# The opening of an adaLN transformer block: modulation loaded in 256, 384 and 384 columns, in row halves, and row tiles normalised on VectorE

## The chip, the cores and the metric

One core of a Trainium2 chip runs the whole program. The metric is the device time of one execution in microseconds, median of the runs. The profile's span (first to last instruction) is 1.9 to 2.0 us shorter than the time of the same execution. All executions but the timed runs of the kernel before in the first comparison were also recorded with their span and their mean granted TensorE clock (1.0 is full speed). A "half clock" below is a stretch in which the trace's clock records say 0.5.

## The reference

The block normalises x, modulates it, runs linear attention with 32 heads, adds the result to x, and does the same again around a SwiGLU network. The part that matters here is the start:

```python
mod = (_silu(c) @ w_mod).reshape(c.shape[0], 6, 1, -1)      # w_mod: 1024 x 6144
sa, ca, ga, sb, cb, gb = (mod[:, 0], mod[:, 1], ...)
h = _layernorm(x, axis=-1) * (1 + ca) + sa                  # x: 2048 x 1024
qkv = h @ wqkv                                              # wqkv: 1024 x 3072
```

So before the first useful product with `wqkv`, the kernel needs part of x normalised and transposed, and part of the rows `sa` and `ca`, each of which is a product of a vector with a 1024 x 1024 matrix (2 MB each).

## The kernel before

The first 512 rows of x (four row tiles of 128) and the K part of `wqkv` (`wk`, 2 MB) are worked on chunk by chunk: chunk `cc` is 128 of the 1024 features. Eight PSUM banks take eight accumulation groups, (row tile, half of K's columns). Bank 7 is at first used for the modulation sums, so group 7 has to wait until the last of them has been read.

```python
def load_wme(p):                       # 256 columns of ca, then 256 of sa, all 1024 rows
    for base in (D, 0):
        s_ = slice(base + p * 256, base + (p + 1) * 256)
        nc.sync.dma_start(out=wme[:, :, s_], in_=wm_v[:, :, s_])
...
load_wme(0); load_wk(0, 2); load_wme(1); load_wk(2, 4)       # written one per line
load_wme(2); load_wk(4, 6); load_wme(3); load_wk(6, 7); load_wk(7, 8)
...
def mod_mm(kind, c0, c1):              # kind 0: ca, kind 1: sa; matmuls with one output column
    for cc in range(c0, c1):
        o = (2 * cc) + kind
        col = (0 if kind else D) + cc * P
        for j in range(DC):
            nc.tensor.matmul(bank[7][:, o:o + 1], lhsT=wme[:, j, col:col + P], rhs=scT[:, j:j + 1],
                             start=(j == 0), stop=(j == DC - 1))
def mod_pair(p):
    mod_mm(0, 2 * p, 2 * p + 2)
    mod_mm(1, 2 * p, 2 * p + 2)
    mod_rows(2 * p, 2 * p + 2)         # casts and + 1 on VectorE
...
for p in (1, 2):
    for cc in (2 * p, 2 * p + 1):
        for g in range(7):
            kmm(bank[g], 0, G[g][0], G[g][1], cc)
            if p == 1 and cc == 3 and g == 2:
                mod_pair(2)
                for c_ in range(4, 6):
                    modulate(0, c_, saT, ca1T)
mod_pair(3)
for cc in range(6, 8):
    modulate(0, cc, saT, ca1T)
spread(nc.vector, scT[:])
for cc in range(6):
    kmm(bank[7], 0, G[7][0], G[7][1], cc)
for g in range(8):
    for cc in range(6, 8):
        kmm(bank[g], 0, G[g][0], G[g][1], cc)
    k_evac(bank[g], *G[g])             # then the V groups follow, and so on for 800 us
```

"Warm" matmuls with zero operands fill TensorE's early waits. "Tail" below means the matmuls that can only run after the last modulation block: here 6 for group 7 and 8 x 2 for chunks 6 and 7, 22 in all, at 216 ns from start to start.

## Time and profile before

| | before |
|---|---|
| time, first three runs | 840.97 us (840.03 to 841.25) |
| the profiled execution | 842.11 us, span 840.2 us, mean clock 0.998 |
| first V matmul (end of the opening) | 32.97 us |

First the page: TensorE's share of the span, and the chain that ended last.

```profile
PE 827.6 (99%) x4144; PEld 389.8 (46%) x4224; DVE 354.4 (42%) x663; ACT 155.0 (18%) x291; POOL 78.9 (9%) x147
...
PE 96%; SPq 1%; DMA 1%; issue 1%; DVE 0%; DVEq 0%
```

TensorE is the bound nearly everywhere. Only the opening has room. Next come TensorE's instructions in order of time (start, duration, engine, source line, operation, operands, count; in brackets the idle time before and what ended it). L197 is a warm matmul, L376 the transposes of a row tile, L391 the modulation matmuls, L271 the K matmuls, L286 the first V matmuls.

```profile
7.78 0.62 PE L376 MATMUL bank<-ident,M 128*128 128x128 bf16 x8 [0.90 <-ACT M L240]
...
11.36 0.62 PE L376 MATMUL bank<-ident,M 128*128 128x128 bf16 x8 [0.64 <-ACT M L240]
11.81 1.03 PE L271 MATMUL bank<-M,M 128*128 128x512 bf16 x3
...
17.04 2.33 PE L271 MATMUL bank<-M,M 128*128 128x512 bf16 x10 [0.24 <-DVE M L253]
19.23 0.55 PE L391 MATMUL bank<-scT,M 128*128 128x1 bf16 x16
20.96 0.55 PE L391 MATMUL bank<-scT,M 128*128 128x1 bf16 x16 [1.18 <-DMA M<-in_w_mod_dram]
...
26.95 0.94 PE L391 MATMUL bank<-scT,M 128*128 128x1 bf16 x32
28.22 4.91 PE L271 MATMUL bank<-M,M 128*128 128x512 bf16 x21 [0.34 <-DVE saT L396]
32.97 7.29 PE L286 MATMUL bank<-M,M 128*128 128x512 bf16 x33
```

The longest wait is 1.18 us, for the third modulation block, whose second transfer landed at 20.92 us. The last group of 21 shown K matmuls (22 were issued; the record of one is missing) is the tail. Then the granted clock: the windows view gives, for each stretch, busy time by engine, and then the granted clock, the share of the DMA engines and GB/s.

```profile
core 0: us, PE busy (x) PEld busy (x) DVE busy (x) ACT busy (x) POOL busy (x), PEclk, DMA share, GB/s
...
20.00:24.00 4.00, 2.82 (x23) 1.30 (x25) 1.10 (x5) 0.00 (x0) 0.00 (x0) 0.76 1.17 306
24.00:28.00 4.00, 3.89 (x43) 2.05 (x42) 0.06 (x1) 0.00 (x0) 0.00 (x0) 0.82 0.99 336
```

The clock is below 1 from 20 to 28 us. The clock records say it exactly: 0.5 from 22.05 us for 3.41 us, and 1.0 for the rest.

The end of the chain of waits:

```profile
826.02 11.11 PE bank L581 x106
```

### The profile page before, as it was taken

The numbers are of one execution on the slowest core, as the hardware profiler recorded it, in microseconds if no ns is written. First come the engines' busy times: TensorE is split into PE (matmuls) and PEld (weight loads), VectorE is DVE, ScalarE is ACT, GpSimd is POOL, SyncE is SP. The second block draws the span as 40 slices with busy tenths as digits, with TensorE's granted clock in tenths as the row PEclk, the third lists the DMA queues.
The fourth block names the chain that finished last, engine by engine and source line by source line (L and its number), as shares of the span: only waits on it lengthen the run. The fifth ranks groups of instructions, "written<-read, shape, count | busy, mean of one in ns | idle before, by whom it ended". The sixth has DMA issues, their size and how long they took to land.

```text
span 840.2 us, 10541 instructions
## 1 busy us (share of the span) xinstructions
PE 827.6 (99%) x4144; PEld 389.8 (46%) x4224; DVE 354.4 (42%) x663; ACT 155.0 (18%) x291; POOL 78.9 (9%) x147
## 2 busy tenths in 40 slices
PE   7999999999999999999999999999999999999998
PEld 3454554544444444444444444444444444444445
DVE  4668888788655656635341111111101211111111
ACT  4335533323211111111110001111000111100000
POOL 2034210022122323100000000000000000000000
PEclk9999999999999999999999999999999999999999
DMA  9985879055599889777874225555322555211210
GB/s 289 312 165 103 161 139 237 17 151 134 127 225 221 219 233 292 187 251 226 249 245 140 76 69 151 151 151 151 106 75 82 154 157 153 76 36 46 76 69 26
DMA packets 223009, 128.62 MB, mean 153 GB/s; under 512 B 76016, under 2 KB 209136, under 8 KB 222960
## 3 DMA queue, kind: packets, MB, share of 16 engines
q1 hardware_dynamic: 182112, 98.58, 43.0%
q10 hardware_dynamic: 38544, 20.98, 11.1%
q0 software_dynamic: 2304, 8.39, 2.6%
q8 instruction: 33, 0.54, 0.3%
q14 instruction: 16, 0.13, 0.1%
HBM read 97.52 MB, written 12.58 MB: 131 GB/s over the span
## 4 chain that ended last, share of the span: by engine, by line
PE 96%; SPq 1%; DMA 1%; issue 1%; DVE 0%; DVEq 0%
PE bank L562 23%; PE bank L581 23%; PE bank L556 23%; PE bank L513 7%; PE bank L286 7%; PE bank L294 7%; PE bank L271 6%; DMA M<-in_w_mod_dram 1%; PE bank L486 1%; PE bank L303 1%; SPq L148 1%; SPq L145 0%; SPq L140 0%; PE bank L391 0%; PE bank L345 0%
## 5 line engine op out<-in xcount | busy, mean ns | idle before, releaser
L562 PE MATMUL bank<-M,M 128*128 128x512 bf16 x881 | 210.4, 379 | 0.9
L556 PE MATMUL bank<-M,M 128*128 128x512 bf16 x870 | 209.5, 379 | 1.3
L564 DVE TENSOR_TENSOR M<-bank,e 128x512 bf16<-128x512 f32 x112 | 77.4, 691 | 249.3 <-PE bank L562 240.8
L581 PE MATMUL bank<-M,M 128*128 128x512 bf16 (+2 forms) x717 | 147.4, 362 | 0.7
L559 ACT ACTIVATE e<-bank 128x512 f32<-128x512 f32 x112 | 66.8, 598 | 436.2 <-PE bank L556 393.7
L581 PEld LDWEIGHTS <-M 128*128 128x128 bf16 x952 | 90.9, 98 | 102.9
L562 PEld LDWEIGHTS <-M 128*128 128x128 bf16 x896 | 87.7, 98 | 105.7
L556 PEld LDWEIGHTS <-M 128*128 128x128 bf16 x896 | 87.3, 98 | 103.8
L584 DVE TENSOR_TENSOR M<-bank,M 128x512 bf16<-128x512 f32 (+2 forms) x34 | 22.4, 660 | 169.9 <-PE bank L581 169.9
L271 PE MATMUL bank<-M,M 128*128 128x512 bf16 x247 | 58.1, 386 | 1.6 <-DVE M L253 0.6
L513 PE MATMUL bank<-M,M 128*128 128x512 bf16 x254 | 57.8, 379 | 0.1
L294 PE MATMUL bank<-M,M 128*128 128x512 bf16 x250 | 56.7, 379 | 0.3
L286 PE MATMUL bank<-M,M 128*128 128x512 bf16 x251 | 55.8, 379 | 0.3
L266 ACT ACTIVATE e<-bank 128x512 f32<-128x512 f32 x64 | 37.3, 596 | 90.2 <-PE bank L294 50.2
L581 PE MATMUL bank<-M 128*128 128x512 bf16 x218 | 50.3, 379 | 0.2
L268 DVE SCALAR_TENSOR_TENSOR M<-bank,e 128x512 bf16<-128x512 f32 x64 | 44.3, 691 | 3.9
L267 DVE TENSOR_SCALAR e<-e 128x512 f32<-128x512 f32 x64 | 29.4, 460 | 23.0 <-ACT e L266 23.0
L271 PEld LDWEIGHTS <-M 128*128 128x128 bf16 x256 | 24.7, 99 | 30.8 <-issue 2.3
L286 PEld LDWEIGHTS <-M 128*128 128x128 bf16 x256 | 25.0, 98 | 30.0
L513 PEld LDWEIGHTS <-M 128*128 128x128 bf16 x256 | 25.0, 98 | 29.7
L294 PEld LDWEIGHTS <-M 128*128 128x128 bf16 x256 | 24.6, 98 | 27.9
L325 DVE CUSTOM_DVE_ANT_0 M<-M,sc_bc 128x1024 f32<-128x1024 bf16 x24 | 29.8, 1241 | 0.5
(84 smaller groups left out, 357.8 us busy)
## 6 DMA issues: line engine op xcount, KB each, us to landing
M<-in_B_w_gate_dram SPq DMA_DIRECT2D x56, 512.0 KB, 3.9
M<-in_B_w_up_dram SPq DMA_DIRECT2D x56, 512.0 KB, 5.1
x_scratch<-M POOLq DMA_DIRECT2D x16, 512.0 KB, 5.8
M<-x_scratch ACTq DMA_DIRECT2D x16, 512.0 KB, 3.4
M<-in_B_w_down_dram SPq DMA_DIRECT2D x6, 1024.0 KB, 8.1
M<-in_A_x_dram SPq DMA_DIRECT2D x16, 256.0 KB, 3.8
M<-in_w_mod_dram SPq DMA_DIRECT2D x8, 512.0 KB, 7.8
M<-in_A_wqkv_dram SPq DMA_DIRECT2D x4, 1024.0 KB, 10.3
```

What stands on the lines that cost most here:

```text
L266: nc.scalar.activation(out=e[:], in_=acc, func=ACT.Exp)
L268: nc.vector.scalar_tensor_tensor(out=dst, in0=acc, scalar=0.0, in1=e[:], op0=ALU.max, op1=ALU.add)
L271: nc.tensor.matmul(acc[:], lhsT=M4[:, sc_, cc, t * P:(t + 1) * P], rhs=wk[:, cc, h * NB:(h + 1) * NB], start=(cc == 0), stop=(cc == DC - 1))
L286: nc.tensor.matmul(acc[:], lhsT=M4[:, sc_, cc, t * P:(t + 1) * P], rhs=wv[:, cc, h * NB:(h + 1) * NB], start=(cc == 0), stop=(cc == DC - 1))
L294: nc.tensor.matmul(acc[:], lhsT=wq[:, cc, qc * P:(qc + 1) * P], rhs=M4[:, sc_, cc, :], start=(cc == 0), stop=(cc == DC - 1))
L325: nc.vector.tensor_tensor_reduce(out=prod.rearrange("p (j k) -> p j k", j=DC), in0=rowT[i][:, :, b, :], in1=sc_bc[:].rearrange("p (j k) -> ...
L513: nc.tensor.matmul(acc[:], lhsT=oTs[st % 3][:, cc, :], rhs=wo[:, cc, hs], start=(cc == 0), stop=(cc == DC - 1))
L556: nc.tensor.matmul(g_ps[:], lhsT=wg_blk[:, cc, fs], rhs=M4[:, sc_, cc, :], start=(cc == 0), stop=(cc == DC - 1))
L559: nc.scalar.activation(out=sg[:], in_=g_ps[:], func=ACT.Silu)
L562: nc.tensor.matmul(u_ps[:], lhsT=wu_blk[:, cc, fs], rhs=M4[:, sc_, cc, :], start=(cc == 0), stop=(cc == DC - 1))
L564: nc.vector.tensor_tensor(out=gus[sc_][:, f, :], in0=u_ps[:], in1=sg[:], op=ALU.mult)
L581: nc.tensor.matmul(y_ps[:, 0:w], lhsT=gus[sc_][:, f, t * P:(t + 1) * P], rhs=wd(f)[:, c0:c1], start=(f == 0), stop=(f == FC - 1))
```

## The change

The intent is to get the modulation in sooner. After the first block of 256 columns come two of 384 (packets of 768 bytes in place of 512, one block fewer), each in two halves of the rows, and the first half is summed while the second still comes in. Row tiles 1 to 3 are normalised on VectorE, which is faster at it than ScalarE, and the PSUM evacuations of row tiles 0 to 2 go to ScalarE.

```diff
+    PH = [(0, 2), (2, 5), (5, 8)]
-    def load_wme(p):
+    def load_wme(p, j0, j1):
         for base in (D, 0):
-            s_ = slice(base + p * 256, base + (p + 1) * 256)
-            nc.sync.dma_start(out=wme[:, :, s_], in_=wm_v[:, :, s_])
+            s_ = slice(base + PH[p][0] * P, base + PH[p][1] * P)
+            nc.sync.dma_start(out=wme[:, j0:j1, s_], in_=wm_v[:, j0:j1, s_])
...
-    load_wme(0)
+    load_wme(0, 0, DC)
     load_wk(0, 2)
-    load_wme(1)
-    load_wk(2, 4)
-    load_wme(2)
-    load_wk(4, 6)
-    load_wme(3)
-    load_wk(6, 7)
-    load_wk(7, 8)
+    load_wme(1, 0, 4)
+    load_wme(1, 4, 8)
+    load_wk(2, 3)
+    load_wk(3, 5)
+    load_wme(2, 0, 4)
+    load_wme(2, 4, 8)
+    load_wk(5, 6)
+    load_wk(6, 8)
...
+    ln_xn(1, nc.vector)          # and tiles 2 and 3 likewise; before: on ScalarE
...
+    kblk(range(7), 2)
+    kblk(range(7), 3)
+    kblk(range(3), 4)
+    mod_mm(2, 0, 0, 4)           # block, kind, rows: first row half
+    mod_mm(2, 1, 0, 4)
+    kblk(range(3, 7), 4)
+    mod_mm(2, 0, 4, 8)           # second row half
+    mod_mm(2, 1, 4, 8)
+    mod_finish(2)
+    modulate_phase(2)
     spread(nc.vector, scT[:])
-    for cc in range(6):
-        kmm(bank[7], 0, G[7][0], G[7][1], cc)
+    for cc in range(5):
+        kblk((7,), cc)
     for g in range(8):
-        for cc in range(6, 8):
-            kmm(bank[g], 0, G[g][0], G[g][1], cc)
+        for cc in range(5, 8):
+            kblk((g,), cc)
         k_evac(bank[g], *G[g])
```

The tail grows: 5 for group 7 and 8 x 3 for chunks 5 to 7, 29 matmuls in place of 22. With halves, several sums are open in bank 7 at once, and only the first matmul of a block carries the start flag. That the sums come out right this way no run tested by itself; the results of the changed kernel (after_again) and of the nine experiments built on it were correct.

More of the change, by code (lines that the diff above doesn't have):

```diff
@@ L196, in warm @@
         for _ in range(n):
-            nc.tensor.matmul(bank[7][:], lhsT=zt[:, 0:P], rhs=zt, start=True, stop=True)
+            nc.tensor.matmul(bank[3][:], lhsT=zt[:, 0:P], rhs=zt, start=True, stop=True)
     stat = {}
@@ L232, in ln_stats_act, with ln_xn @@
         stat[st] = (rstd, nmr)
-    def ln_xn(st, pool):
+    def ln_xn(st, eng=None):
         rstd, nmr = stat.pop(st)
-        if pool:
-            nc.gpsimd.tensor_scalar(out=xns[st % 6], in0=xs[st % 6], scalar1=rstd[:], scalar2=nmr[:],
-                                    op0=ALU.mult, op1=ALU.add)
+        if eng is not None:
+            eng.tensor_scalar(out=xns[st % 6], in0=xs[st % 6], scalar1=rstd[:], scalar2=nmr[:],
+                              op0=ALU.mult, op1=ALU.add)
         else:
@@ L246, in ln @@
             ln_stats(st)
-        ln_xn(st, True)
+        ln_xn(st, nc.gpsimd)
         sc_, t = divmod(st, STC)
@@ L380, in tr0_evac @@
         dst = M4[:, 0, :, st * P:(st + 1) * P]
-        if st % 2 == 0:
+        if st < 3:
             nc.scalar.copy(out=dst, in_=tp)
@@ L384, in tr0_evac, with mod_mm @@
             nc.vector.tensor_copy(out=dst, in_=tp)
-    def mod_mm(kind, c0, c1):
-        for cc in range(c0, c1):
-            o = (2 * cc) + kind
-            col = (0 if kind else D) + cc * P
-            for j in range(DC):
+    def mod_mm(p, kind, j0, j1):
+        c0, c1 = PH[p]
+        for j in range(j0, j1):
+            for cc in range(c0, c1):
+                o = (2 * cc) + kind
+                col = (0 if kind else D) + cc * P
                 nc.tensor.matmul(bank[7][:, o:o + 1], lhsT=wme[:, j, col:col + P], rhs=scT[:, j:j + 1],
-                                 start=(j == 0), stop=(j == DC - 1))
+                                 start=(not kind and j == 0 and cc == c0),
+                                 stop=(kind == 1 and j == DC - 1 and cc == c1 - 1),
+                                 skip_group_check=True)
     def mod_rows(c0, c1):
@@ L397, in mod_rows, with mod_finish, modulate_phase @@
         nc.vector.tensor_scalar_add(out=ca1T[:, c0:c1], in0=m1[:, 1, c0:c1], scalar1=1.0)
-    def mod_pair(p):
-        mod_mm(0, 2 * p, 2 * p + 2)
-        mod_mm(1, 2 * p, 2 * p + 2)
-        mod_rows(2 * p, 2 * p + 2)
-    warm(17)
-    for st in range(STC):
-        ln_stats(st)
+    def mod_finish(p):
+        mod_rows(*PH[p])
+    def modulate_phase(p, c0=0, c1=SCW):
+        for cc in range(*PH[p]):
+            modulate(0, cc, saT, ca1T, c0, c1)
+    warm(19)
     mask = const.tile([P, KVW], BF16, name="mask")
@@ L413 @@
     nc.gpsimd.memset(v_c[:, :, :, P:VW], 1.0)
-    ln_xn(0, False)
+    for st in range(3):
+        ln_stats(st)
+    ln_xn(0)
     tr0(0)
-    warm(3)
-    ln_xn(1, False)
-    tr0(1)
-    tr0_evac(0)
-    ln_xn(2, False)
-    ln_xn(3, False)
+    tr0_evac(0)
+    warm(2)
+    ln_xn(1, nc.vector)
+    tr0(1)
+    tr0_evac(1)
+    ln_stats(3)
+    mod_mm(0, 0, 0, DC)
+    mod_mm(0, 1, 0, DC)
+    warm(3)
+    mod_finish(0)
+    modulate_phase(0, 0, 2 * P)
+    for st in (2, 3):
+        ln_xn(st, nc.vector)
     load_cols(wv, 2 * D, 0)
@@ L427, with kblk @@
     load_cols(wq, 0, 1)
-    tr0_evac(1)
-    mod_pair(0)
+    G = [(t, h) for t in range(STC) for h in range(NH)]
+    def kblk(gs, cc):
+        for g in gs:
+            kmm(bank[g], 0, G[g][0], G[g][1], cc)
+    kblk(range(4), 0)
     tr0(2)
     tr0_evac(2)
-    for cc in range(2):
-        modulate(0, cc, saT, ca1T, 0, 2 * P)
-    G = [(t, h) for t in range(STC) for h in range(NH)]
-    for cc in range(2):
-        for g in range(4):
-            kmm(bank[g], 0, G[g][0], G[g][1], cc)
-        if cc == 0:
-            tr0(3)
-            tr0_evac(3)
-            for c_ in range(2):
-                modulate(0, c_, saT, ca1T, 2 * P, 4 * P)
-    for cc in range(2):
-        for g in range(4, 7):
-            kmm(bank[g], 0, G[g][0], G[g][1], cc)
-        if cc == 0:
-            mod_pair(1)
-            for c_ in range(2, 4):
-                modulate(0, c_, saT, ca1T)
-    for p in (1, 2):
-        for cc in (2 * p, 2 * p + 1):
-            for g in range(7):
-                kmm(bank[g], 0, G[g][0], G[g][1], cc)
-                if p == 1 and cc == 3 and g == 2:
-                    mod_pair(2)
-                    for c_ in range(4, 6):
-                        modulate(0, c_, saT, ca1T)
-    mod_pair(3)
-    for cc in range(6, 8):
-        modulate(0, cc, saT, ca1T)
+    kblk(range(2), 1)
+    tr0(3)
+    tr0_evac(3)
+    kblk(range(2, 4), 1)
+    modulate_phase(0, 2 * P, 4 * P)
+    mod_mm(1, 0, 0, 4)
+    mod_mm(1, 1, 0, 4)
+    kblk(range(4, 7), 0)
+    mod_mm(1, 0, 4, 8)
+    mod_mm(1, 1, 4, 8)
+    mod_finish(1)
+    modulate_phase(1)
+    kblk(range(4, 7), 1)
+    kblk(range(7), 2)
[8 more added lines that the diff above has]
+    modulate_phase(2)
     spread(nc.vector, scT[:])
-    for cc in range(6):
-        kmm(bank[7], 0, G[7][0], G[7][1], cc)
+    for cc in range(5):
+        kblk((7,), cc)
     for g in range(8):
-        for cc in range(6, 8):
-            kmm(bank[g], 0, G[g][0], G[g][1], cc)
+        for cc in range(5, 8):
+            kblk((g,), cc)
         k_evac(bank[g], *G[g])
```

## The prediction

> **What bounds the kernel now.** The page shows TensorE busy 99% of 840.2 us, and the chain that ended last is 96% TensorE. The waits view shows no TensorE wait after 33 us. So only the opening can move: from 0 to 32.97 us, when the first V matmul starts (TensorE timeline). There the DMA queue runs full (about 290 to 390 GB/s in every microsecond from 3 us on, by the windows view) and TensorE waits in small pieces: 0.90 and 0.27 us (normalised x), 0.64 us (row 2 on ScalarE), 0.38 and 0.24 us (modulation on VectorE), then 1.18 us at 19.8 to 20.96 for the third modulation block. From 22.05 to 25.46 us the granted clock is 0.5, one stretch of 3.41 us that costs 3.41/2 = 1.7 us of TensorE work. The stretch just before it held that wait and N=1 matmuls. [...]
>
> **What changes.**
> 1. Modulation columns 256+256+256+256 become 256+384+384, each 384 in two row halves. DMA packets grow from 512 to 768 bytes. Landings before: 256-column blocks take 3.4 to 4.5 us per MB, wk with 2 KB packets 2.8 us per MB, wv with 1 KB packets 3.0. I estimate 3.25 us per MB for 768 bytes: 3 MB of modulation save about 1.8 us. The last modulation byte lands at about 23.0 to 23.7 us (before: 25.72), the last wk at about 25.3 (before: 27.09).
> 2. After the last landing only 24 N=1 matmuls remain (0.6 us), since the first half was summed already. The K tail after them is 5+24 matmuls at 216 ns = 6.3 us (before: 6+16 = 4.75 us): more tail, but no work in front of it waits.
> 3. Row tiles 1 to 3 are normalised on VectorE: ScalarE takes 1.24 us per tile; on VectorE I estimate 0.54 us, from modulation 0.344 us at 256 and 0.410 us at 512 columns. Evacuations 0 to 2 go to ScalarE (0.99 us), 3 to VectorE (0.69 us). Stats of row 3 now come after row 1's normalisation, so the first modulation still ends near 11.5 to 11.8 us. First K matmul: 11.5 to 11.8 us, before 11.81. No gain there.
> 4. Warm matmuls 20 become 24, in gaps, free. One set of casts and adds less (0.4 us of VectorE), not critical.
>
> **Sum.** After: block 1 finished about 16.6 us, K blocks dense from 17.5 us, second half of block 2 ends about 23.3, bank 7 free about 23.8, 29 matmuls to about 30.2 to 30.5 us. Before: 32.97. Gain 2.3 to 2.7 us against the profiled run, if the half clock disappears: about 1.2 us of it is the clock stretch, the rest earlier landings and the vanished 1.18 us wait. Where runs of before escape the half clock, before would be limited by the landing at 25.72 and the gain is about 1.5 us. Everything after is TensorE-bound and merely moves forward.
>
> **Prediction.** 838.7 us, 80% range 837.2 to 840.4. Faster by over 2%: 0.3%; within 2%: 99%; slower: 0.7%.
>
> **What would show it.** First V matmul at 30 to 31 us; no clock record of 0.5 after 6 us; no TensorE wait over 0.8 us on the modulation load; last modulation landing under 24 us; VectorE normalisation about 0.54 us; TensorE still without waits after 33 us.
>
> **What would make it wrong.** 768-byte packets no faster per byte; a half-clock stretch in the after run (more N=1 matmuls lie together, and its tiles wait around 14 to 17 us); the wait for bank 7 between block 2's reads and the last K group; the K evacuations or the wv load (before landed 29.99 us) now too late for the earlier V groups.

## The result

| | before | changed |
|---|---|---|
| time, median of 6 runs each | 840.62 us (840.03 to 841.25) | 839.83 us (839.22 to 840.41) |
| the profiled execution | 842.11 us, span 840.2, clock 0.998 | 839.79 us, span 837.9, clock 1.000 |
| first K matmul | 11.81 us | 11.53 us |
| last modulation transfer lands | 25.72 us | 23.78 us |
| first V matmul | 32.97 us | 30.86 us |

The ratio is 0.999, with a 95% interval of 0.9977 to 1.0003. The two profiled executions differ by 842.11 - 839.79 = 2.3 us, the medians by 0.8 us.

The page of the changed kernel:

```profile
PE 827.3 (99%) x4148; PEld 390.2 (47%) x4228; DVE 354.6 (42%) x662; ACT 153.2 (18%) x289; POOL 79.5 (9%) x147
...
PE 96%; SPq 2%; DMA 1%; issue 1%; DVE 0%; DVEq 0%
```

TensorE's timeline. Lines have moved: L200 warm, L379 transposes, L395 modulation, L274 K, L289 V.

```profile
7.71 0.62 PE L379 MATMUL bank<-ident,M 128*128 128x128 bf16 x8
...
11.53 1.04 PE L274 MATMUL bank<-M,M 128*128 128x512 bf16 x4 [0.25 <-DVE M L256]
...
15.36 0.59 PE L274 MATMUL bank<-M,M 128*128 128x512 bf16 x2 [0.46 <-DVE M L256]
...
17.62 3.84 PE L274 MATMUL bank<-M,M 128*128 128x512 bf16 x17 [0.24 <-DVE M L256]
21.30 0.74 PE L395 MATMUL bank<-scT,M 128*128 128x1 bf16 x24
...
22.76 0.44 PE L395 MATMUL bank<-scT,M 128*128 128x1 bf16 x12
23.82 0.45 PE L395 MATMUL bank<-scT,M 128*128 128x1 bf16 x12 [0.62 <-DMA M<-in_w_mod_dram]
24.60 6.42 PE L274 MATMUL bank<-M,M 128*128 128x512 bf16 x28 [0.32 <-DVE saT L402]
30.86 9.44 PE L289 MATMUL bank<-M,M 128*128 128x512 bf16 x43
```

The wait for the last block is 0.62 us now, and the tail (28 of its 29 matmuls recorded) takes 6.4 us in place of 4.9. The windows view of the changed kernel shows a full clock:

```profile
core 0: us, PE busy (x) PEld busy (x) DVE busy (x) ACT busy (x) POOL busy (x), PEclk, DMA share, GB/s
...
20.00:24.00 4.00, 3.31 (x53) 2.10 (x53) 0.00 (x0) 0.00 (x0) 0.00 (x0) 1.00 1.08 354
24.00:28.00 4.00, 3.68 (x28) 1.77 (x25) 2.84 (x9) 1.38 (x3) 0.00 (x0) 1.00 1.10 362
```

And the end of the chain:

```profile
823.91 11.11 PE bank L595 x106
```

Subtract the first V matmul from the start of this last chain piece: 826.02 - 32.97 = 793.05 us before, 823.91 - 30.86 = 793.05 us after. From the first V matmul on, the two executions agree to 10 ns. The same sum, taken from each of the 14 traces (first V matmul to the end of TensorE's last), lies between 804.14 and 804.19 us. So nothing is given back later. The time of the first V matmul tells everything about a run but what follows TensorE's last matmul (the last evacuation and store), which took 2.8 to 3.1 us.

### The profile page after: what moved, and what is told of

Its sections match the earlier page's. It is cut to its first block, busy times and chain, and to the rows that moved or that the text cites. A ratio compares the mean times of both kernels' runs of the same rounds, so it can differ in the third digit from the quotient of the medians. Undisturbed runs are those within 1.5% of the kernel's fastest.

```text
span 837.9 us, 10535 instructions
## 1 busy us (share of the span) xinstructions
PE 827.3 (99%) x4148; PEld 390.2 (47%) x4228; DVE 354.6 (42%) x662; ACT 153.2 (18%) x289; POOL 79.5 (9%) x147
## 3 DMA queue, kind: packets, MB, share of 16 engines
q0 software_dynamic: 2304, 8.39, 2.6%
## 4 chain that ended last, share of the span: by engine, by line
PE 96%; SPq 2%; DMA 1%; issue 1%; DVE 0%; DVEq 0%
PE bank L576 23%; PE bank L595 23%; PE bank L570 23%; PE bank L527 7%; PE bank L289 7%; PE bank L297 7%; PE bank L274 6%; DMA M<-in_w_mod_dram 1%; PE bank L500 1%; PE bank L306 1%; SPq L147 1%; SPq L150 1%; SPq L140 0%; PE bank L348 0%; DVE M L361 0%
## 5 line engine op out<-in xcount | busy, mean ns | idle before, releaser
L274 PE MATMUL bank<-M,M 128*128 128x512 bf16 x248 | 56.6, 379 | 1.7 <-DVE M L256 1.0
L289 PE MATMUL bank<-M,M 128*128 128x512 bf16 x251 | 55.8, 379 | 0.3
L289 PEld LDWEIGHTS <-M 128*128 128x128 bf16 x256 | 25.0, 98 | 30.0
L274 PEld LDWEIGHTS <-M 128*128 128x128 bf16 x256 | 24.3, 98 | 29.3 <-DVE M L256 1.8
```

What stands on the lines that cost most here:

```text
L274: nc.tensor.matmul(acc[:], lhsT=M4[:, sc_, cc, t * P:(t + 1) * P], rhs=wk[:, cc, h * NB:(h + 1) * NB], start=(cc == 0), stop=(cc == DC - 1))
L289: nc.tensor.matmul(acc[:], lhsT=M4[:, sc_, cc, t * P:(t + 1) * P], rhs=wv[:, cc, h * NB:(h + 1) * NB], start=(cc == 0), stop=(cc == DC - 1))
```

## The experiments

Twelve experiments ran, each for five timed rounds beside the kernel before, on three chips; all were correct. The two theories at the start:

- Theory 1: the profiled execution of the kernel before was an unlucky one with a half clock. At full clock the changed kernel gains little, because the opening ends at the last modulation landing plus the tail, and the tail grew by 7 x 0.216 = 1.5 us while the landing came earlier.
- Theory 2: the half clock is the rule in the kernel before, and the changed kernel gives its gain back later. (The equal 793.05 us speak against the second half already.)

### before_again: the kernel before once more

The edit is none.

> The kernel before, unchanged, as a control. Theory 1 (the profiled execution of before, 842.11 us, was an unlucky one with a half-clock stretch, and most executions have none): most runs lie at 840.0 to 841.3 us, a profile that shows no clock record of 0.5 after 6 us has its first V matmul at about 31.5 us (landing of the last modulation block 25.7 + 0.2 of its matmuls after it + 0.8 for casts and the freeing of bank 7 + 22 matmuls at 216 ns = 4.75) and not at 32.97. Theory 2 (the half clock is in most executions of before, and the change's gain is given back later): the profile shows the 0.5 stretch again and the first V matmul at about 33 us. Ratio to before 1.000 within 0.001.

The median was 841.09 us (840.25 to 842.58), ratio 1.0009 (0.9997 to 1.0022). The profile fell on a full-clock execution of 840.25 us:

```profile
20.47 0.55 PE L391 MATMUL bank<-scT,M 128*128 128x1 bf16 x16 [0.66 <-DMA M<-in_w_mod_dram]
...
24.96 1.02 PE L391 MATMUL bank<-scT,M 128*128 128x1 bf16 x32
26.32 4.91 PE L271 MATMUL bank<-M,M 128*128 128x512 bf16 x21 [0.34 <-DVE saT L396]
31.07 9.23 PE L286 MATMUL bank<-M,M 128*128 128x512 bf16 x41
```
```profile
core 0: us, PE busy (x) PEld busy (x) DVE busy (x) ACT busy (x) POOL busy (x), PEclk, DMA share, GB/s
20.00:24.00 4.00, 3.45 (x29) 1.69 (x31) 1.10 (x5) 0.00 (x0) 0.00 (x0) 1.00 1.17 306
24.00:28.00 4.00, 3.61 (x45) 2.10 (x44) 1.70 (x6) 0.00 (x0) 0.00 (x0) 1.00 1.08 356
```
```profile
824.16 11.11 PE bank L581 x106
```

Here the third block's second transfer landed at 20.42 us instead of 20.92, the wait was 0.66 us instead of 1.18, the clock stayed full, and the V matmuls started at 31.07 us, 1.9 us earlier than in the first profile. Both traces have nearly the same phase of the clock records (first record at 4.98 and 4.94 us), so the phase is not what differs; the visible difference is half a microsecond in the landing of that transfer. That it decided the clock is argued from this one pair of traces. The V matmuls are also 0.4 us earlier than Theory 1 had put them, which comes up again below.

All executions of the kernel before that were recorded with span and clock are 41. In 28 of them the clock is 0.999 or 1.000, with spans of 838.3 to 839.1 us, median 838.6. Eight have 0.998 and spans of 840.2 to 840.6. Five have 0.997 or 0.998 and yet 838.7 to 838.9; where their clock was lower no trace shows. Theory 1 holds on this point: the half clock that makes an execution 1.6 to 2.0 us longer than that median struck 8 of 41 executions, and the first profile, which is not among the 41, was one such.

### after_again: the changed kernel once more

The edit is none.

> The changed kernel, unchanged, for a closer interval on one chip with the others. Theory 1: ratio to before 0.9985 to 0.9995, that is 0.4 to 1.2 us less, first V matmul at 30.5 to 31.3 us, no half clock, no TensorE wait after 33 us. Theory 2: the same opening, but TensorE waits or a lower clock later in the run that the kernel before has not.

Median 839.84 us (839.47 to 841.69), ratio 0.9995 (0.9981 to 1.0009), first V matmul at 30.89 us. Of the 11 recorded executions of the changed kernel ten have a clock of 1.000, with spans of 837.3 to 838.5, median 837.9; one has 0.998 and 839.8. So at full clock the changed kernel is ahead by 838.6 - 837.9 = 0.7 us in the medians. On the chip of this submission alone it is 838.5 - 837.75 = 0.75 us. The interval of the ratio includes 1; a single half clock in five runs is larger than the gain. In the two full-clock traces before_again and changed the gain of the opening alone is 31.07 - 30.86 = 0.2 us.

### before_fill: the wait before the half clock, filled

```diff
     def mod_pair(p):
         mod_mm(0, 2 * p, 2 * p + 2)
+        if p == 2:
+            for _ in range(5):
+                nc.tensor.matmul(bank[7][:, 32:NB], lhsT=zt[:, 0:P], rhs=zt[:, 32:NB], start=True, stop=True)
```

> The kernel before with five warm matmuls of 480 columns (about 1.0 us at full clock) between the two kinds of the third modulation pair, where TensorE waited 1.18 us. Theory 1: the wait shrinks to under 0.3 us, no clock record of 0.5 after 6 us, first V matmul at 31.3 to 31.8 us; the time equals that of before within 0.5 us, since most executions of before have no half clock to lose. Theory 2: it is 1.0 us or more faster than before.

Median 840.56 us (840.29 to 840.97), ratio 1.000 (0.9988 to 1.0013), first V matmul at 31.15 us, no 0.5 record before the end, and the wait of 1.18 us is gone. All five executions were at 0.999 or 1.000. This agrees with Theory 1 and contradicts Theory 2: without the half clock the kernel before takes what its median execution takes. It does not show that the fill is what kept the clock: at 8 in 41, five executions in a row escape by chance about one time in three (an estimate). The first V matmul came 0.15 us earlier than expected.

### whole_rows: no row halves

```diff
-    load_wme(1, 0, 4)
-    load_wme(1, 4, 8)
+    load_wme(1, 0, DC)
...
-    mod_mm(2, 0, 0, 4)
-    mod_mm(2, 1, 0, 4)
     kblk(range(3, 7), 4)
-    mod_mm(2, 0, 4, 8)
-    mod_mm(2, 1, 4, 8)
+    mod_mm(2, 0, 0, DC)
+    mod_mm(2, 1, 0, DC)
```

(Block 1 and the load of block 2 likewise.)

> The changed kernel without row halves: each 384-column block is loaded in two transfers of all rows and summed when both have landed. Theory 1: the landing of the last block stays at 23.5 to 24.2 us; after it come 24 N=1 matmuls of the second kind instead of 12, 0.3 us more, so the first V matmul is at 31.0 to 31.5 us, 0.2 to 0.6 us later than in the changed kernel. A rival, that the halves are what brought the gain: first V matmul at 31.7 us or later, no gain left against before.

Median 840.42 us (840.2 to 841.17), ratio 0.9999 (0.9987 to 1.0012). The profile fell on the one execution of five with a half clock (17.65 to 21.06 us), with the first V matmul at 31.99 us, so it cannot be compared with the changed kernel's. The other four executions have spans of 838.3 to 838.6, median 838.5: 0.6 us longer than the changed kernel's 837.9, at the upper edge of the expectation. The last landing was at 23.73 us as expected. An estimate from the spans (838.5 less 804.15 and about 2.95 us) puts the first V matmul at full clock at about 31.4 us, short of the rival's 31.7. But the rival's other mark was met: beside the full-clock executions of the kernel before in the same submission, also 838.5, no gain is left. Taken out of the changed kernel, the halves are worth about 0.6 us. (The parts do not add up: the wide blocks and the VectorE move, taken out in the same way below, cost 0.4 to 0.6 us each, though the whole change gains 0.7 us. So none of the parts can be called the one that gains.)

### norm_act: row tiles 1 to 3 on ScalarE

```diff
-    ln_xn(1, nc.vector)
+    ln_xn(1)
...
     for st in (2, 3):
-        ln_xn(st, nc.vector)
+        ln_xn(st)
```

> The changed kernel with row tiles 1, 2 and 3 normalised on ScalarE again. Theory 1 (the opening ends at the last modulation landing plus a tail of fixed length): the first K matmul slips from 11.5 to about 12.6 us and block 1 is summed about 0.6 us later, but TensorE's wait of 0.6 to 0.7 us for the last landing at about 23.8 us takes it up: first V matmul at 30.8 to 31.3 us, time within 0.4 us of the changed kernel where the clock stays full. A half-clock stretch is likelier, since TensorE idles about 1 us more between 9.6 and 13 us. The rival (the move to VectorE is what gains): first V matmul at 31.8 us or later without a half clock.

Median 841.57 us (841.47 to 842.03), ratio 1.0009 (0.9995 to 1.0023). All five executions had a clock of 0.998, so the half clock was not only "likelier" but came every time, and my main number (30.8 to 31.3 us) failed: the first V matmul was at 32.41 us.

```profile
10.58 0.62 PE L379 MATMUL bank<-ident,M 128*128 128x128 bf16 x8 [1.81 <-ACT M L243]
...
13.09 1.91 PE L274 MATMUL bank<-M,M 128*128 128x512 bf16 x4
...
32.41 1.89 PE L289 MATMUL bank<-M,M 128*128 128x512 bf16 x8
```

TensorE waits 1.81 us for row tile 1, because ScalarE first evacuates row tile 0 and then normalises (1.24 us against 0.54 us on VectorE). From 11.60 to 15.01 us the clock record is 0.5. Two causes are mixed in this run, the later start and the clock; a later run, told next, parts them.

### norm_fill: the same, but that wait filled

```diff
-    warm(2)
+    warm(10)
```

> The changed kernel with row tiles 1 to 3 on ScalarE, as in the earlier run, but ten warm matmuls in place of two in the wait for row tile 1 (1.8 us), so that this wait earns no half clock. Theory 3 (what the move to VectorE is worth is the full clock, since the later start alone is taken up by the wait for the last landing): no half clock in most executions, first V matmul at 30.8 to 31.4 us, 1.0 us or more earlier than the 32.41 without the fill, span 837.8 to 838.5. Its rival (the later start is lost time by itself): first V matmul at 31.8 us or later at full clock.

Median 840.2 us (840.11 to 840.71), ratio 0.9991 (0.9977 to 1.0005), all five clocks 1.000.

```profile
8.23 2.32 PE L200 MATMUL bank<-M 128*128 128x512 bf16 x10
10.64 0.62 PE L379 MATMUL bank<-ident,M 128*128 128x128 bf16 x8
...
12.96 1.04 PE L274 MATMUL bank<-M,M 128*128 128x512 bf16 x4 [0.25 <-DVE M L256]
...
31.34 2.97 PE L289 MATMUL bank<-M,M 128*128 128x512 bf16 x13
```

With the wait filled, the first V matmul comes at 31.34 us, 1.07 us before norm_act's and 0.48 us after the changed kernel's. The K matmuls started 12.96 - 11.53 = 1.43 us later, so about 1 us of the late start is taken up by waits further on (the changed kernel's 0.62 us for the last landing is gone from this trace). Since norm_act had the half clock in five of five and this kernel in none, the filled wait is what earned it there. Theory 3, as stated there, holds: most of what the move to VectorE is worth is the full clock, and only 0.4 to 0.5 us is the earlier start.

### blocks256: four blocks of 256 columns, with halves

```diff
-    PH = [(0, 2), (2, 5), (5, 8)]
+    PH = [(0, 2), (2, 4), (4, 6), (6, 8)]
```

(Loads, sums and the tail of 6 + 16 follow from it.)

> The changed kernel with four blocks of 256 columns, row halves kept. Theory 1: the last landing comes later, at 25.2 to 25.6 us, as in the kernel before, but 22 instead of 29 matmuls follow it: landing 25.4 + 0.25 of sums + 0.5 to free bank 7 + 4.75 = 30.7 to 31.1 us for the first V matmul, the same as the changed kernel within 0.3 us: the wider blocks won nothing in net. The rival (larger packets and the earlier landing are what gains): first V matmul 1.5 us or more later than in the changed kernel.

Median 840.34 us (840.31 to 840.58), ratio 0.9993 (0.998 to 1.0005), all five clocks 1.000, first V matmul at 31.17 us, last landing at 25.38 us.

```profile
25.56 0.54 PE L397 MATMUL bank<-scT,M 128*128 128x1 bf16 x16
26.42 4.91 PE L276 MATMUL bank<-M,M 128*128 128x512 bf16 x22 [0.32 <-DVE saT L404]
31.17 3.19 PE L291 MATMUL bank<-M,M 128*128 128x512 bf16 x14
```

The last landing is 1.6 us later than in the changed kernel, and the opening ends only 0.3 us later. The span medians differ by 838.5 - 837.9 = 0.6 us (measured on different chips). So the wide blocks do not bring the 1.6 us of their earlier landing: what they win at the landing they mostly lose in the longer tail. The rival, 1.5 us or more, is refuted.

### mid512 and mid512_fill: the small block last

If landing plus tail were all, blocks of 256, 512 and 256 columns should win on both counts.

```diff
-    PH = [(0, 2), (2, 5), (5, 8)]
+    PH = [(0, 2), (2, 6), (6, 8)]
```

> The changed kernel with blocks of 256, 512 and 256 columns: the last block is small again, so 22 matmuls follow it, while 2 MB of the 4 still move in packets of 768 bytes or more. Theory 1: block 1 is summed by about 17.6 us, 42 K matmuls then keep TensorE busy to about 24.3 us, the last landing is at 23.8 to 24.5 us, and the first V matmul comes at 29.5 to 30.1 us; time 0.8 to 1.4 us less than the changed kernel. If the tail did not matter: first V matmul at 30.9 us or later.

Median 840.26 us (839.99 to 840.89), ratio 0.9993 (0.9981 to 1.0006). Two of five executions had 0.998, the profile among them (first V matmul 31.97 us). The three at full clock have spans of 838.1 to 838.4, no better than the changed kernel, where I had expected 0.8 to 1.4 us less. One fault was mine: the K weights of chunks 3 to 5 were one transfer, which landed at 21.30 us. The second kernel mends that and the half clock:

```diff
-    load_wk(3, 6)
+    load_wk(3, 4)
+    load_wk(4, 6)
...
     mod_mm(1, 0, 4, 8)
+    fill(4)        # zero weights, start=False, onto a running K sum: adds nothing
     mod_mm(1, 1, 4, 8)
```

> Blocks of 256, 512 and 256 columns again, with two mends: the K weights of chunks 3 to 5 are loaded as 3 and then 4 and 5 (in the earlier trace the three together landed at 21.3 us, while TensorE could have used the first at 19.2), and four matmuls with zero weights, which add nothing to a running sum, lie in the wait for block 1's last transfer, where the half clock was earned. Theory 1 (last landing plus tail, once the clock is full): no clock record of 0.5, last landing at 23.8 to 24.7 us, first V matmul at 29.9 to 30.6 us, time 0.3 to 0.9 us less than the changed kernel, all clocks 1.0. If the first V matmul is again at 31 us or later at full clock, the tail is not what counts and theory 1 is wrong for this kernel.

Median 839.96 us (839.69 to 840.42), ratio 0.9987 (0.9975 to 1.000), all five clocks 1.000. The last landing was at 24.36 us as expected, but the first V matmul of the profiled execution, the slowest of the five, at 31.56 us:

```profile
19.50 5.35 PE L275 MATMUL bank<-M,M 128*128 128x512 bf16 x24 [0.24 <-DVE M L257]
24.69 0.54 PE L396 MATMUL bank<-scT,M 128*128 128x1 bf16 x16
...
25.96 0.54 PE L396 MATMUL bank<-scT,M 128*128 128x1 bf16 x16
26.82 4.91 PE L275 MATMUL bank<-M,M 128*128 128x512 bf16 x22 [0.32 <-DVE saT L403]
31.56 2.75 PE L290 MATMUL bank<-M,M 128*128 128x512 bf16 x12
```

TensorE did not wait for the last block: the block landed at 24.36 us, and TensorE reached its first sums at 24.69 us and the last at 25.96 us. From 19.50 us on it worked without a pause but for the 0.3 us for bank 7. So Theory 1's "landing plus tail" is wrong as a general rule. It describes the changed kernel, where TensorE waits for the last landing; in this one TensorE itself is late, because block 1 (2 MB here) landed only at 17.99 us.

### last512: the large block last

```diff
-    PH = [(0, 2), (2, 5), (5, 8)]
+    PH = [(0, 2), (2, 4), (4, 8)]
```

> The reverse: blocks of 256, 256 and 512 columns, so 4 + 32 = 36 matmuls follow the last block. Theory 1: the landing is at 23.4 to 24.2 us, no earlier than in the changed kernel by more than 0.4, and the first V matmul comes at 31.9 to 32.7 us, 1.0 to 1.8 us later than in the changed kernel, and TensorE waits 2 us or more for the last block, so that a half clock in some executions adds up to 1.7 us.

Median 842.26 us (840.88 to 842.52), ratio 1.0012 (1.0000 to 1.0025). Four of five executions had 0.998 (spans 840.1 to 840.6), one 0.999 (839.0). Here TensorE waits for the block (landed 22.99 us, earlier than I had expected) and the tail of 36 matmuls follows from 23.93 us; the profiled execution had its half clock from 23.28 to 26.69 us, and its first V matmul at 33.04 us. An estimate for full clock is 23.93 + 36 x 0.216 = 31.7 us. The wait shown before the last transfer's sums is 0.95 us, half of what I had expected.

### after_fill: the changed kernel with its two waits filled

```diff
     mod_mm(1, 1, 0, 4)
+    fill(2)
...
     mod_mm(2, 0, 4, 8)
+    fill(2)
     mod_mm(2, 1, 4, 8)
```

> The changed kernel with two zero-weight matmuls in each of its two waits of about half a microsecond (before the first use of row tile 3, and before the last modulation transfer). Only the clock should change: no execution at 0.998, spans 837.5 to 838.3 as the full-clock executions of the changed kernel had, which showed one of 0.998 and 839.8 in five on the first chip.

Median 839.87 us (839.65 to 840.01), ratio 0.9986 (0.9973 to 0.9998), all five clocks 1.000, spans 837.8 to 838.1. It is as fast as the changed kernel at full clock. Five runs are too few to show that it never falls to the half clock, where the changed kernel did once in 11.

### last128: an attempt to beat both

```diff
-    PH = [(0, 2), (2, 5), (5, 8)]
+    PH = [(0, 2), (2, 5), (5, 7), (7, 8)]
```

(With the fill of row tile 3's wait, and with two K matmuls moved behind each last sum.)

> An attempt at a kernel that beats both: blocks of 256, 384, 256 and 128 columns in the changed kernel, two zero-weight matmuls in the wait for row tile 3, and only 7 + 8 = 15 matmuls after the last block instead of 29. TensorE work from the first K matmul (11.5 us) adds up to about 17.1 us, so 28.6 us is the earliest possible end of the opening. Theory 1 (landing plus tail, with TensorE's own work as a floor): if the 128-column block (packets of 256 bytes) lands by 26 us, the first V matmul comes at 30.0 to 30.6 us and the time is 0.3 to 0.9 us less than the changed kernel's. If packets of 256 bytes cost much more per byte, the landing passes 26.5 us and the gain is gone. The rival that the tail is not what counts: no earlier first V matmul although the landing is by 26 us.

Median 840.25 us (839.76 to 840.9), ratio 0.9992 (0.9979 to 1.0006), all clocks 1.000. The last block landed at 25.41 us, inside the condition, and yet the first V matmul came at 31.06 us:

```profile
11.83 1.04 PE L275 MATMUL bank<-M,M 128*128 128x512 bf16 x4 [0.25 <-DVE M L257]
...
26.42 0.54 PE L396 MATMUL bank<-scT,M 128*128 128x1 bf16 x16
26.82 3.87 PE L275 MATMUL bank<-M,M 128*128 128x512 bf16 x17
31.06 3.18 PE L290 MATMUL bank<-M,M 128*128 128x512 bf16 x14 [0.36 <-DVE M L272]
```

TensorE reached the last block's sums at 26.42 us, one microsecond after they could have run. Then the tail was so short that two new waits appeared: the first V group needs bank 0, which VectorE was still reading (0.36 us of idle, L272), and the V weights, which landed at 30.89 us against 28.77 us in the changed kernel. It does not beat the changed kernel. None of my versions does, beyond the noise.

### What the traces have in common

A count of TensorE's work between the first K matmul and the first V matmul: 64 K matmuls at 0.216 us, 96 modulation matmuls at 0.025 us and the transposes at 0.056 us each (start to start, from the trace). It is an estimate, and it can be set beside the measured stretch:

```
trace (full clock)   first K   first V   stretch   work counted   rest
before_again          11.88     31.07     19.19     16.7            2.5
after                 11.53     30.86     19.33     17.1            2.2
blocks256             11.53     31.17     19.64     17.1            2.5
norm_fill             12.96     31.34     18.38     17.1            1.3
mid512_fill           12.15     31.56     19.41     17.1            2.3
after_fill            11.42     31.07     19.65     17.1            2.5
```

(The changed kernel transposes one row tile more after its first K matmul, hence 17.1 and not 16.7; mid512_fill and after_fill have 4 fill matmuls, 0.9 us, in their rest.) By this estimate the whole opening can win about 2 us at most after the first K matmul, at full clock, and the rest consists of three or four short waits: for row tile 3, for the casts and the modulation of a block, for the landing, for bank 7. TensorE waits about as long for a landing as before (0.66 us for the third block in before_again, 0.62 us for the last one now), and the other waits moved about. That TensorE's own work is the floor was argued from these counts; no run took work away from it.

## Why the prediction was right or wrong

The measured 839.83 us lies in the stated range of 837.2 to 840.4, 1.1 us above the point. By the points:

- "Everything after is TensorE-bound and merely moves forward": right, to 10 ns (793.05 us in both).
- "First K matmul: 11.5 to 11.8 us": right, 11.53. The VectorE estimate of 0.54 us: right, 0.541 us. The 3.25 us per MB for 768-byte packets: right, the 384 KB transfers landed 1.20 us apart, 3.2 us per MB.
- "The last modulation byte lands at about 23.0 to 23.7 us": 23.78 us. The transfer of K weights before it took 2.1 us instead of 1.4.
- "29 matmuls to about 30.2 to 30.5 us": 30.86 us, 0.4 us late, from that landing.
- "Gain 2.3 to 2.7 us against the profiled run": 2.3 us between the profiled executions, 2.1 us in the first V matmul, so right or just short. Its split was wrong, so part of this is luck: 1.9 of the 2.1 us is the difference between two executions of the kernel before (32.97 and 31.07), where I had put 1.2 us on the clock, and 0.2 us is the change. The step that failed is the next one: the point of 838.7 is that gain subtracted from 840.97 us, the median of the timed runs, although the profiled run, with its half clock, was at 842.11 us. Subtracting the gain from its own base gives 842.11 - 2.3 = 839.8 us, which is what was measured. before_again, before_fill and the count of 8 in 41 show that the half clock belongs to that execution and not to the kernel.
- "Where runs of before escape the half clock ... the gain is about 1.5 us": mis-sized. It is 0.2 us in the two full-clock traces, and 0.7 us in the medians of the full-clock spans. The term that was wrong is the end of the full-clock opening before: I put it at about 31.8 us, it was 31.07, since its last landing came at 25.38 and TensorE got to the block at 24.96, just in time. With 22 matmuls behind it, 25.38 + 5.69 = 31.07; with 29, 23.78 + 7.08 = 30.86: of the 1.6 us of earlier landing, 1.4 us went into the longer path after it. The sums hold in other full-clock traces: before_fill 25.46 + 5.69 = 31.15 (measured 31.15), after_again 23.82 + 7.08 = 30.90 (30.89), after_fill 23.99 + 7.08 = 31.07 (31.07). For the first profile the sum gives 25.72 + 5.69 = 31.4 (an estimate), so of its 1.9 us some 1.6 us is the half clock and 0.3 us a later landing. I had noted the longer tail, but wrote that "no work in front of it waits", while in fact TensorE waited 0.62 us for the landing.
- That the half clock comes from waits and small matmuls was right as far as norm_act and norm_fill test it: with ScalarE doing the normalising in the changed kernel it strikes five of five, and with the wait filled none. Whether the change lowers the risk is not shown: 1 of 11 executions against 8 of 41 is too few to tell.
- That 839.83 us fell inside the range says little for the account: the range lay 0.2 to 3.4 us under the median before (840.62), and the forecast for a full-clock execution, 1.5 us, was twice the 0.7 us measured or more.

## What to carry to other kernels

Before a gain read from a profile is subtracted from a time, check that the profiled execution is typical: compare its own time with the timed runs, and its clock with theirs. Two executions of the same kernel that differed by half a microsecond in one landing differed by a half-clock stretch, and a fill of zero matmuls in a wait is a cheap test of it (norm_act had the half clock in five of five executions, norm_fill in none). An earlier landing pays only what the work behind it leaves over (here 0.2 of 1.6 us): count the work that depends on the last transfer, and count the work of the busy engine in the whole stretch, before the transfers are rearranged.

## What else the traces show: the clock, the packets, the instruction queue

- The half clocks in before (22.05 to 25.46 us), whole_rows (17.65 to 21.06), norm_act (11.60 to 15.01) and last512 (23.28 to 26.69) all lasted 3.41 us, and in before the record of 1.0 in front of it lasted 17.07 us, five times as long. So windows of 3.41 us are compared here: those just before each half clock, and some that kept the clock, counted from the traces (large = 512 columns; wait = the longest inside the window, in us; a record or two may be missing):

```
trace          window         large  transposes  1-column  wait   then
before         18.63-22.05      6        0          32     1.18   0.5
whole_rows     14.24-17.65      5        0          48     0.81   0.5
mid512         13.78-17.19      4        0          48     0.84   0.5
last512        19.86-23.28      4        0          45     0.95   0.5
norm_act        8.18-11.60      1        8          23     1.81   0.5
norm_fill      15.50-18.92      7        0          48     0.24   1.0
before_again   18.59-22.01      8        0          32     0.66   1.0
after_again    13.07-16.48      5        8          48     0.46   1.0
before          8.39-11.81      2       16          32     0.64   1.0
before          4.98- 8.39      9        8           0     0.90   1.0
```

  The five windows before a half clock held 1 to 6 large matmuls and a wait of 0.81 to 1.81 us. The last row shows that a wait of 0.90 us alone did not cost the clock: that window held 9 large matmuls. How one-column matmuls count for the clock is not shown. Here 45 to 48 of them in a window with 4 or 5 large matmuls (whole_rows, mid512, last512) did not keep it.
- The rows after_again and before 8.39 show windows that kept the full clock with 8 or 16 transposes and only 5 or 2 large matmuls, beside waits of 0.46 and 0.64 us. How transposes count for the clock no run tested.
- Loading from HBM was slower here with smaller packets: 202 GB/s from 23 to 24 us in last128, where nearly all packets had 256 bytes, 292 GB/s from 22 to 23 us in before with 512-byte packets, 326 GB/s from 19 to 21 us in the changed kernel with 768-byte packets, and 354 GB/s with packets of 1 and 2 KB (blocks256, 24 to 25 us). The landings hide the loss in last128 (1.06 and 0.75 us after the transfer before, for 256 KB each), since these packets had begun at 21.35 us beside the transfer before. 384 KB in 768-byte packets took 1.20 us.
- In five traces (before, changed, norm_act, blocks256, mid512) a 16 KB packet on the instruction queue, begun between 16.5 and 18.7 us, ran for 1.1 to 1.2 us, and a data transfer landing within 3.1 us of its start came 0.5 to 1.3 us later than its size explains. Other traces speak against it: beside the packet at 17.05 us in last128 nothing landed more than 0.2 us late, and in mid512_fill a transfer landed about 1 us late at 10.62 us with no such packet near. It is a coincidence in time; whether such a packet delays a data transfer no run tested.
